# Square into a spent tile, first state over ScalarE and GpSimd, a third output tile

## The chip, the cores and the metric

The kernel runs on one core of a Trainium2 chip. Its engines work from queues of their own and wait for each other by semaphores: TensorE (PE) multiplies matrices, VectorE (DVE) and ScalarE (ACT) work on rows of SBUF and PSUM, GpSimd (POOL) on SBUF alone in this kernel, and SyncE (SP) issues every transfer. The metric is the device time of one execution in microseconds (us).

## The reference

Three stages follow each other, on 4 batches of 768 positions:

- Gated linear attention, 8 heads of 48: `state = alpha[t] * state + k[t] v[t]^T`, `y[t] = q[t] state`.
- A spectral mix: `theta = x @ w_theta`, `zr = x cos(theta)`, `zi = x sin(theta)`, `y = w_tok_r zr + w_tok_i zi` over positions, `u = x + y`, then `u + relu(u @ w_ch)`. Width 384.
- A gated convolution: `h = relu(x @ w_in)` (1024 wide), a depthwise convolution of three taps over positions, a sigmoid gate, and `(h * gate) @ w_out`.

All is in float32, and the weights are stored as 64-bit words.

## The kernel before

**Attention.** Positions are cut into 6 chunks of 128 per batch, 24 chunks in all. For each chunk DVE makes products of decay factors: a backward scan (line 210) and, from its inverse at the chunk's start, a forward scan (line 215), both into one tile `fbt`, of which there is one. Line 218 multiplies them into q and k. ScalarE then squares the tile in place (line 219) for the sake of a row sum, `bacc`, with which the kernel later finds whether any factor overflowed. The decay factors come in a tile `a_t`, of which there are two; nothing reads its first 512 columns after the forward scan. `ftot`, four numbers a row (line 216), is the chunk's whole decay.

TensorE makes the scores `sc`, ScalarE copies them into `pt` (line 232), GpSimd masks them (line 233), TensorE makes `y` from pt and v and, from the second chunk of a batch on, from the running state `S`. `kv` (line 264) is the chunk's own addition to the state. From the second chunk on, DVE sums S and kv into `tst` (line 268) and GpSimd multiplies with the next chunk's decay (line 273), in two instructions, one for either half of the heads. In a batch's first chunk there is no sum, and DVE multiplies kv straight out of PSUM. Two state tiles alternate. `x` is the copy of y, `xps` and `u` its transpose.

**Spectral mix.** `th` is theta; its chain runs over ScalarE and DVE (lines 310 to 315) to the tile `zf`, which is split in a high part `zh` (ScalarE) and a low part `zl` (DVE, line 72), since each product of matrices is done in three passes of such halves (`mm3`). The mix `yps` of a batch takes 18 matmuls for each of 6 chunks and each half of the positions; the token weights of the first half are `wtok00`, `wtok01`, those of the second `wtok10`, `wtok11`. The matmuls of a batch's mix stand among those of the next batch's attention. For batch 0 there is no earlier mix to fill in.

**Weights.** Each piece of a weight is loaded into a tile `stage` (two of them), decoded by DVE (lines 101 to 103) and split: the cast by ScalarE (line 71), the rest by DVE (line 72). w_theta takes two pieces, w_tok 12, of which the first six are the first half of the positions.

**Last stage.** `hps`, `ops` and `cps` are the products with w_in, w_out and w_ch. ScalarE copies each finished output into a tile `ob` (line 492), of which there are two, and SyncE stores it.

**The order.** It is not written out by hand: the program is handed to a scheduler, which simulates a timeline of it and sets each engine's queue by that. Each engine then goes through its queue in order. An edit of one instruction so moves others on all engines.

Of the kernel before, what the change touches and what calls it, by code (L numbers as in the profile page):

```python
# [8 lines left out]
F32 = mybir.dt.float32  # L9
F32R = mybir.dt.float32r  # L10
BF16 = mybir.dt.bfloat16
# [3 lines left out]
AF = mybir.ActivationFunctionType  # L15
# [3 lines left out]
P = 128  # L19
B, H, S, D = 4, 8, 768, 48  # L20
DM = H * D
# [7 lines left out]
CW = 4 * P  # L29
# [14 lines left out]
def tile_gated_linear_attention__then__spectral_moe__then__conv_gate(  # L44
# [14 lines left out]
    nc = tc.nc  # L59
    NCH = B * NC  # L60

    def mm(o, lhsT, rhs, start, stop):
        nc.tensor.matmul(o, lhsT, rhs, start=start, stop=stop, skip_group_check=True)  # L63

    def mm3(o, a, b, start, stop):
        mm(o, a[0], b[0], start, False)
        mm(o, a[0], b[1], False, False)
        mm(o, a[1], b[0], False, stop)
# [8 lines left out]
    bacc = top_p.tile([P, NCH], F32, name="bacc")  # L77
# [7 lines left out]
    def body(top, slow):  # L85
# [38 lines left out]
        with ExitStack() as ph1:  # L124
# [73 lines left out]
            def a_prep(ci):  # L198
                at, qt, vt = raw.pop(ci)
                qr = qt[:, 0:CW]  # L200
                kr = qt[:, CW : 2 * CW]
                ff = at[:, 0:CW]
                ash = at[:, 1 : CW + 1]
                ast = at[:, CW + 1 : CW + 5]
                fbt = sc_p.tile([P, 2, CW], F32, tag="fbt", name="fbt")
                fo, bf = fbt[:, 0], fbt[:, 1]
                bt = bf.rearrange("p (a t) -> p a t", a=4)
                of = onehot.rearrange("p a t -> p (a t)")
                ftot = att.tile([P, 4], F32, tag="ftot", name="ftot")
                nc.vector.tensor_tensor_scan(  # L210
                    bf[:, CW - 1 :: -1], ash[:, CW - 1 :: -1], of[:, CW - 1 :: -1], 0.0, ALU.mult, ALU.add
                )
                nc.vector.tensor_scalar(starts[:, :, 0], bt[:, :, 0], LEAST, None, ALU.max)
                nc.vector.reciprocal(starts[:, :, 0], starts[:, :, 0])
                nc.vector.tensor_tensor_scan(fo, ff, starts.rearrange("p a t -> p (a t)"), 0.0, ALU.mult, ALU.add)  # L215
                nc.vector.tensor_tensor(ftot, ast, bt[:, :, 0], ALU.mult)
                fl = fbt.rearrange("p b t -> p (b t)")
                nc.vector.tensor_tensor(qt, qt, fl, ALU.mult)  # L218
                nc.scalar.activation(fl, fl, AF.Square, accum_out=bacc[:, ci : ci + 1])  # L219
                prep[ci] = (qr.rearrange("p (a t) -> p a t", a=4), kr.rearrange("p (a t) -> p a t", a=4), ftot, vt)  # L220

            def a_score(ci):
# [21 lines left out]
            def a_y(ci):  # L244
                qh, kh, ftot, vt = prep.pop(ci)
                pts, kt = scored.pop(ci)
                c = ci % NC
                Sp, Sn = Sst[ci % 2], Sst[(ci + 1) % 2]
                y = ps_a.tile([P, DM], F32, tag="a", name="y")
                first = True  # L250
                for p in range(NP):
                    for j in range(2):
                        h = 2 * p + j
                        mm(y[:, h * D : (h + 1) * D], pts[j][:, p, :], vt[:, h * D : (h + 1) * D], first, c == 0)
                        first = False
                    if c > 0:
                        mm(y[:, p * 96 : p * 96 + 96], qh[:, p, :], Sp[:, p, :], False, True)
                x = x_p.tile([P, DM], F32, tag="x", name="x")
                nc.scalar.copy(x, y)
                xs[ci] = x  # L260
                if c < NC - 1:
                    kv = ps_a.tile([P, NP, 2 * D], F32, tag="a", name="kv")
                    for p in range(NP):
                        mm(kv[:112, p, :], kt[:, p, :112], vt[:, p * 96 : p * 96 + 96], p == 0, True)
                    nft = prep[ci + 1][2]
                    if c > 0:
                        tt = att.tile([P, NP, 2 * D], F32, tag="tst", name="tst", bufs=1)
                        nc.vector.tensor_tensor(tt[:112], Sp[:112], kv[:112], ALU.add)
                    else:
                        tt = kv  # L270
                    for j in range(2):
                        r = slice(64 * j, 64 * j + D)
                        (nc.gpsimd if c > 0 else nc.vector).tensor_tensor(  # L273
                            Sn[r, :, j * D : (j + 1) * D],
                            tt[r, :, j * D : (j + 1) * D],
                            nft[r].unsqueeze(2).to_broadcast([D, NP, D]),
                            ALU.mult,
                        )
# [64 lines left out]
            def a_att(b, c):  # L343
                ci = b * NC + c
                if slow:
                    xs[ci] = x_p.tile([P, DM], F32, tag="x", name="x")
                    nc.sync.dma_start(out=xs[ci], in_=x_dram[b, c * P : (c + 1) * P, :])
                    a_xt(ci)
                    return
                if ci + 2 < NCH:  # L350
                    a_load(ci + 2)
                if ci + 1 < NCH:
                    a_prep(ci + 1)
                    a_score(ci + 1)
                a_y(ci)
                a_xt(ci)

            if not slow:
                a_load(0)
                a_load(1)  # L360
                wps = ps_a.tile([P, 512], F32, tag="a", name="wps")
                for _ in range(NWARM):
                    nc.tensor.matmul(wps, onehot[:, 0, :], onehot.rearrange("p a t -> p (a t)"), start=True, stop=True)
                a_prep(0)
                a_score(0)
# [79 lines left out]
        mlp = top.enter_context(tc.tile_pool(name="mlp", bufs=2))  # L445
# [39 lines left out]
        def m_out(b, h, i):  # L485
            ps = ps_n.tile([P, 512], F32, tag="n", name="ops")
            ts_ = slice(i * P, (i + 1) * P)
            for f in range(NF):
                g = gsp[b, h, f]
                mm3(ps[:, :DM], (g[:, 0, ts_], g[:, 1, ts_]), (wout[0][:, f, :], wout[1][:, f, :]), f == 0, f == NF - 1)  # L490
            ob = mlp.tile([P, DM], F32, tag="ob", name="ob")
            nc.scalar.activation(ob, ps[:, :DM], AF.Copy, scale=0.5)
            t0 = h * HALF + i * P
            nc.sync.dma_start(out=out[b, t0 : t0 + P, :], in_=ob)
# [43 lines left out]
        for n, (b, h) in enumerate(units):  # L538
            if n > 0:
                m_xsplit(b, h)  # L540
            for f in range(NF):
                m_in(b, h, f)
                if n > 0 and f in (1, 3, 5):
                    m_out(*units[n - 1], f // 2)
                i = NF * n + f - 2 * NF
                if not slow and i % 2 and 0 <= i // 2 < NTOP:
                    top_min(i // 2)
                if f == 6 and n + 2 < len(units):
                    m_usplit(*units[n + 2])
                    m_ch(*units[n + 2], ps_m, "m")  # L550
            if n == 7 and not slow:
                count_bad()
        for i in range(3):
            m_out(*units[-1], i)
# [102 lines left out]
```

## Time and profile before

| | us |
|---|---|
| median of 3 runs | 613.31 |
| lowest, highest run | 610.01, 613.78 |
| the profiled execution, its own time | 610.02 |
| its span, first to last instruction | 608.3 |
| PE busy | 584.0 (96%) |
| DVE busy | 459.9 (76%) |
| ACT busy | 333.3 (55%) |
| POOL busy | 71.1 (12%) |

Shares are means over stages that differ. The profile tells the busy time of each engine by stretches of the span, the chain of work that ended last, what each engine waited for, and groups of instructions by line, operation and shape. A matmul in float32 appears as two in the trace. The granted clock is TensorE's, 1.00 being 2.4 GHz.

### The profile page before, as it was taken

The page shows a single profiled execution, that of the slowest core. Times are in us where ns is not written, and L with a number is a line of the kernel's source. Part 1 is how long each engine was busy: PE and PEld are TensorE (multiplying, and loading weights), DVE is VectorE, ACT ScalarE, POOL GpSimd, SP SyncE. Part 2 cuts the span into 40 slices and gives each one's busy share as a digit, 9 for nine tenths or more (in the row PEclk, how much of TensorE's full clock was granted, in tenths as well). Part 3 has the DMA queues.
Part 4 walks back from the last instruction along what each step waited for, and adds up shares of the span by engine and source line. Part 5 has one row for each costly group of instructions (what it writes and reads, how often), then busy time and mean ns, then how long its engine had stood idle before and what let it go on. Part 6 is the DMA issues. An engine that isn't in the chain of part 4 may idle for free.

```text
span 608.3 us, 9546 instructions
## 1 busy us (share of the span) xinstructions
PE 584.0 (96%) x3703; PEld 569.2 (94%) x3703; DVE 459.9 (76%) x744; ACT 333.3 (55%) x663; POOL 71.1 (12%) x91
## 2 busy tenths in 40 slices
PE   5789999899999999999999999999999999999996
PEld 2689888799999999999999999999999999999995
DVE  7699999976764567643156888998888888888781
ACT  3436766444682446733265343666776767766571
POOL 1023621432001330112100000000000000000000
PEclk8557899899999999999999999999999999999999
DMA  8356464343102431021001333430023535445111
GB/s 297 116 176 215 151 222 127 125 138 112 62 19 77 131 119 48 15 66 61 1 0 74 110 106 105 122 138 13 27 79 117 194 118 182 148 152 194 55 41 44
DMA packets 24981, 65.33 MB, mean 107 GB/s; under 512 B 2528, under 2 KB 8672, under 8 KB 24544
## 3 DMA queue, kind: packets, MB, share of 16 engines
q1 hardware_dynamic: 24928, 64.64, 32.3%
q8 instruction: 31, 0.51, 0.3%
q14 instruction: 22, 0.18, 0.1%
HBM read 59.92 MB, written 4.72 MB: 106 GB/s over the span
## 4 chain that ended last, share of the span: by engine, by line
PE 83%; DVE 11%; DMA 2%; issue 1%; ACT 1%; POOL 1%; ACTq 0%; DVEq 0%
PE yps L63 23%; PE hps L63 17%; PE ops L63 16%; PE y L63 8%; PE cps L63 6%; PE th L63 5%; PE sc L63 3%; PE kv L63 2%; DMA stage<-in_w_tok_dram 2%; DVE fbt L215 2%; DVE fbt L210 1%; PE kps L239 1%; DVE qk_t L218 1%; DVE stage L102 1%; DVE wtok L72 1%
## 5 line engine op out<-in xcount | busy, mean ns | idle before, releaser
L63 PE MATMUL yps<-wtok,zh 128*128 128x384 f32 x576 | 151.6, 343 | 1.0 <-ACT zh L71 1.0
L63 PEld LDWEIGHTS yps<-wtok,zh 128*128 128x128 f32 x576 | 105.9, 192 | 1.7 <-ACT zh L71 1.4
L63 PE MATMUL hps<-x,win 128*128 128x386 f32 x576 | 107.1, 339 | 0.0
L63 PE MATMUL ops<-wout,g 128*128 128x384 f32 x576 | 106.9, 338 | 0.0
L63 PEld LDWEIGHTS hps<-x,win 128*128 128x128 f32 x576 | 102.2, 189 | 0.0
L63 PEld LDWEIGHTS ops<-wout,g 128*128 128x128 f32 x576 | 101.7, 187 | 0.0
L63 PE MATMUL yps<-wtok,zl 128*128 128x384 f32 x288 | 97.9, 344 | 0.0
L233 POOL TENSOR_SCALAR_AFFINE_SELECT pt<-pt 128x512 f32<-128x512 f32 x48 | 46.0, 981 | 214.9 <-ACT pt L232 214.9
L63 PE MATMUL y<-v_t,pt 128*128 128x48 f32 x384 | 59.2, 286 | 0.0
L63 PEld LDWEIGHTS y<-v_t,pt 128*128 128x128 f32 x384 | 56.3, 213 | 0.5
L63 PEld LDWEIGHTS yps<-wtok,zl 128*128 128x128 f32 x288 | 55.2, 192 | 0.0
L219 ACT ACTIVATE fbt<-fbt 128x1024 f32<-128x1024 f32 x24 | 25.4, 1059 | 52.8 <-DVE qk_t L218 52.5
L479 ACT ACTIVATE cv<-cv 128x384 f32<-128x384 f32 x64 | 33.4, 523 | 31.0 <-DVE cv L476 30.9
L72 DVE TENSOR_TENSOR g<-cv,g 128x384 fp32r<-128x384 f32 x64 | 35.4, 555 | 15.1 <-ACT g L71 14.5
L63 PE MATMUL th<-wth,zh 128*128 128x384 f32 x216 | 44.3, 348 | 0.0
L232 ACT COPY pt<-sc 128x512 f32<-128x512 f32 x48 | 25.7, 585 | 29.7 <-PE y L63 29.7
L210 DVE TENSOR_TENSOR_SCAN fbt<-a_t,onehot 128x512 f32<-128x512 f32 x24 | 29.7, 1236 | 16.3 <-ACT fbt L219 14.4
L63 PEld LDWEIGHTS sc<-qk_t 48*128 48x128 f32 x384 | 28.6, 204 | 14.0 <-issue 7.5
L63 PE MATMUL sc<-qk_t 48*128 48x128 f32 x384 | 33.8, 304 | 8.0 <-DVE qk_t L218 8.0
L473 DVE SCALAR_TENSOR_TENSOR cv<-hh,cw,cv 128x383 f32<-128x383 f32 (+1 forms) x64 | 38.3, 612 | 4.1 <-ACT cv L470 3.8
L63 PE MATMUL y<-S,qk_t 128*128 128x96 f32 x160 | 37.5, 319 | 3.9 <-POOL S L273 3.9
L480 DVE SCALAR_TENSOR_TENSOR cv<-cv,hh 128x384 f32<-128x384 f32 x64 | 35.2, 555 | 7.9 <-ACT cv L479 5.9
(84 smaller groups left out, 903.5 us busy)
## 6 DMA issues: line engine op xcount, KB each, us to landing
qk_t<-in_qka_dram SPq DMA_DIRECT2D x24, 512.0 KB, 3.7
stage<-in_w_tok_dram SPq DMA_DIRECT2D x12, 768.0 KB, 4.9
top<-in_w_tok_dram SPq DMA_DIRECT2D x12, 768.0 KB, 4.3
a_t<-in_qka_dram SPq DMA_DIRECT2D x24, 260.0 KB, 2.8
v_t<-in_v_dram SPq DMA_DIRECT2D x24, 192.0 KB, 3.3
out_dram<-ob SPq DMA_DIRECT2D x24, 192.0 KB, 1.9
stage<-in_w_in_dram SPq DMA_DIRECT2D x4, 768.0 KB, 5.1
stage<-in_w_out_dram SPq DMA_DIRECT2D x4, 768.0 KB, 4.3
```

The lines of the kernel that those rows point to most:

```text
L63: nc.tensor.matmul(o, lhsT, rhs, start=start, stop=stop, skip_group_check=True)
L72: lo_eng.tensor_tensor(lo, src, hi.bitcast(F32), ALU.subtract)
L102: nc.vector.scalar_tensor_tensor(fb, hi, 0xC0000000, fb, ALU.bitwise_and, ALU.bitwise_or)
L210: nc.vector.tensor_tensor_scan(bf[:, CW - 1 :: -1], ash[:, CW - 1 :: -1], of[:, CW - 1 :: -1], 0.0, ALU.mult, ALU.add)
L215: nc.vector.tensor_tensor_scan(fo, ff, starts.rearrange("p a t -> p (a t)"), 0.0, ALU.mult, ALU.add)
L218: nc.vector.tensor_tensor(qt, qt, fl, ALU.mult)
L219: nc.scalar.activation(fl, fl, AF.Square, accum_out=bacc[:, ci : ci + 1])
L232: nc.scalar.copy(pt, scs[j])
L233: nc.gpsimd.affine_select(pt, pt, [[0, NP], [1, P]], ALU.is_ge, 0.0, base=0, channel_multiplier=-1)
L473: nc.vector.scalar_tensor_tensor(cv[:, a:HALF], hh[:, o + a - 1 : o + HALF - 1], cw[:, f, 0:1], cv[:, a:HALF], ALU.mult, ALU.add)
L479: nc.scalar.activation(cv, cv, AF.Tanh, scale=0.5)
L480: nc.vector.scalar_tensor_tensor(cv, cv, 1.0, hh[:, o : o + HALF], ALU.add, ALU.mult)
```

## The change

Three edits. The Square writes its result, which nobody reads, as bfloat16 into the first 512 columns of `a_t`, and stands ahead of the product with q and k; both now only read `fbt`. In a batch's first chunk ScalarE copies the two blocks of kv into the state tile, and GpSimd multiplies them there in place. `ob` has three tiles.

```diff
@@ a_prep
                 fl = fbt.rearrange("p b t -> p (b t)")
+                sink = at[:, 0:CW].bitcast(BF16)
+                nc.scalar.activation(sink, fl, AF.Square, accum_out=bacc[:, ci : ci + 1])
                 nc.vector.tensor_tensor(qt, qt, fl, ALU.mult)
-                nc.scalar.activation(fl, fl, AF.Square, accum_out=bacc[:, ci : ci + 1])
@@ a_y
                     else:
-                        tt = kv
+                        tt = Sn
+                        for j in range(2):
+                            r = slice(64 * j, 64 * j + D)
+                            nc.scalar.copy(Sn[r, :, j * D : (j + 1) * D], kv[r, :, j * D : (j + 1) * D])
                     for j in range(2):
                         r = slice(64 * j, 64 * j + D)
-                        (nc.gpsimd if c > 0 else nc.vector).tensor_tensor(
+                        nc.gpsimd.tensor_tensor(
@@ m_out
-            ob = mlp.tile([P, DM], F32, tag="ob", name="ob")
+            ob = mlp.tile([P, DM], F32, tag="ob", name="ob", bufs=3)
```

In the changed kernel the product of line 218 is line 220; the lines behind it are one higher, and four higher from the state products (now line 277) on. On DVE, the opening of batch 0, from the third chunk's reciprocal on, stood so before:

```order
L273 TENSOR_TENSOR S1_112<-kv_234,ftot_192 48x4x48 x2
L215 SCALAR_TENSOR_TENSOR fbt_276<-a_t_185,starts_110 128x512
L72 TENSOR_TENSOR wth1_116<-stage_247,wth0_115 128x768
L218 TENSOR_TENSOR qk_t_187<-qk_t_187,fbt_276 128x1024
L72 TENSOR_TENSOR wth1_116<-stage_255,wth0_115 128x384
L72 TENSOR_TENSOR zh_344<-u_241,zh_344 128x384
L210 SCALAR_TENSOR_TENSOR fbt_373<-a_t_270,onehot_109 128x512
```

and stands so now:

```order
L215 SCALAR_TENSOR_TENSOR fbt_278<-a_t_185,starts_110 128x512
L220 TENSOR_TENSOR qk_t_187<-qk_t_187,fbt_278 128x1024
L72 TENSOR_TENSOR wth1_116<-stage_249,wth0_115 128x768
L210 SCALAR_TENSOR_TENSOR fbt_375<-a_t_272,onehot_109 128x512
L213 TENSOR_SCALAR starts_110<-fbt_375 128x4
L216 TENSOR_TENSOR ftot_376<-a_t_272,fbt_375 128x4
L72 TENSOR_TENSOR wth1_116<-stage_257,wth0_115 128x384
```

The state products are gone; the product with q and k stands ahead of the split of the theta weights, and the next chunk's scan right behind that split. On ScalarE the queue now reads there, from the first chunk's kt on:

```order
L242 COPY kt_183<-kps_178 128x512
L242 COPY kt_221<-kps_216 128x512
L274 COPY S1_112<-kv_234 48x4x48 x2
L115 ACTIVATE stage_249<-stage_249 128x768
L233 COPY pt_210<-sc_200 128x512
L233 COPY pt_213<-sc_201 128x512
L260 COPY x_232<-y_223 128x384
L71 CAST wth0_115<-stage_249 128x768
L115 ACTIVATE stage_257<-stage_257 128x384
L219 ACTIVATE a_t_185,bacc_61<-fbt_278 128x1024
```

Before, the cast of the theta weights stood between the two pt, two places behind the scaling of line 115; now kt, both copies into the state, both pt and x stand ahead of it. The third place is DVE in the middle of batch 0, from chunk 0's zl on. Before:

```order
L72 TENSOR_TENSOR zl_364<-zf_357,zh_344 128x768
L216 TENSOR_TENSOR ftot_568<-a_t_464,fbt_567 128x4
L72 TENSOR_TENSOR zh_538<-u_241,zh_538 128x384
L311 SCALAR_TENSOR_TENSOR zf_454<-zf_454,th_444 128x384
L218 TENSOR_TENSOR qk_t_466<-qk_t_466,fbt_567 128x1024
L101 TENSOR_SCALAR stage_621<-stage_621 128x768
L101 TENSOR_SCALAR stage_709<-stage_709 128x768
L102 SCALAR_TENSOR_TENSOR stage_621<-stage_621 128x768
L315 TENSOR_TENSOR zf_454<-x_321,zf_454 128x768
```

Now:

```order
L72 TENSOR_TENSOR wtok01_85<-stage_436,wtok00_84 128x2x384
L103 SCALAR_TENSOR_TENSOR stage_533<-stage_533 128x768
L72 TENSOR_TENSOR zl_366<-zf_359,zh_346 128x768
L72 TENSOR_TENSOR wtok01_85<-stage_533,wtok00_84 128x2x384
L101 TENSOR_SCALAR stage_623<-stage_623 128x768
L102 SCALAR_TENSOR_TENSOR stage_623<-stage_623 128x768
L269 TENSOR_TENSOR tst_427<-S0_111,kv_422 112x384
L103 SCALAR_TENSOR_TENSOR stage_623<-stage_623 128x768
L101 TENSOR_SCALAR stage_711<-stage_711 128x768
L216 TENSOR_TENSOR ftot_570<-a_t_466,fbt_569 128x4
L102 SCALAR_TENSOR_TENSOR stage_711<-stage_711 128x768
L72 TENSOR_TENSOR wtok01_85<-stage_623,wtok00_84 128x2x384
```

Where the theta chain of chunk 1 (lines 311 and 315, zf_454) stood right behind chunk 0's zl, the decodes of the fifth and sixth piece of w_tok (stage_623, stage_711) stand now, and the theta chain behind them.

## Rows read from the trace of the kernel before

**Rows 1.** Busy us (count) by stretch: PE, PEld, DVE, ACT, POOL; granted clock, DMA share, GB/s.

```profile
40.00:60.00 20.00, 20.00 (x118) 18.97 (x117) 19.59 (x29) 11.85 (x23) 7.15 (x6) 0.67 0.77 254
...
100.00:120.00 20.00, 17.46 (x138) 16.51 (x138) 19.89 (x29) 9.87 (x19) 7.27 (x6) 0.95 0.46 139
120.00:300.00 180.00, 180.00 (x1338) 174.56 (x1336) 105.81 (x158) 89.18 (x173) 35.07 (x52) 0.99 0.23 72
```

**Rows 2.** The chain that ended last: start us, us, what.

```profile
17.93 2.91 PE y L63 x14
...
99.36 1.03 PE kv L63 x8
...
103.57 2.83 PE y L63 x24
...
107.19 3.18 PE yps L63 x18
...
112.13 0.56 DVE tst L268
...
112.77 2.69 POOL S L273
...
116.69 3.55 PE y L63 x20
```

**Rows 3.** Waits of DVE, 0 to 40 us: us in total, times, longest.

```profile
DVE stage L101 <- DMA stage<-in_w_tok_dram: 1.7, 1, 1.7
DVE fbt L210 <- ACT fbt L219: 1.5, 2, 1.2
```

**Rows 4.** DVE in order of time: start us, us, instruction, idle before and releaser.

```profile
21.77 0.72 DVE L273 TENSOR_TENSOR S<-kv,ftot 48x192 f32<-48x192 f32 x2 [3.24 <-PE kv L63]
```

**Rows 5.** ACT by form, 0 to 120 us: busy us, mean ns, idle before and releaser.

```profile
L219 ACT ACTIVATE fbt<-fbt 128x1024 f32<-128x1024 f32 x10 | 10.6, 1058 | 26.6 <-DVE qk_t L218 26.6
...
L241 ACT COPY kt<-kps 128x512 f32<-128x512 f32 x8 | 4.8, 597 | 1.5 <-PE kps L239 1.1 <-PE kv L63 0.4
L259 ACT COPY x<-y 128x384 f32<-128x384 f32 x8 | 3.9, 489 | 0.0
...
L71 ACT CAST wth<-stage 128x768 fp32r<-128x768 f32 x1 | 0.8, 835 | 0.0
```

**Rows 6.** DVE by form, 0 to 120 us.

```profile
L210 DVE TENSOR_TENSOR_SCAN fbt<-a_t,onehot 128x512 f32<-128x512 f32 x11 | 13.7, 1245 | 3.4 <-DMA a_t<-in_qka_dram 1.9 <-ACT fbt L219 1.5
L103 DVE SCALAR_TENSOR_TENSOR stage<-stage 128x768 uint32<-128x768 uint32 x13 | 12.6, 973 | 0.0
...
L102 DVE SCALAR_TENSOR_TENSOR stage<-stage 128x768 uint32<-128x768 uint32 x13 | 12.5, 960 | 0.0
L72 DVE TENSOR_TENSOR wtok<-stage,wtok 128x768 fp32r<-128x768 f32 x11 | 11.5, 1048 | 0.0
L101 DVE TENSOR_SCALAR stage<-stage 128x768 uint32<-128x768 uint32 x13 | 7.8, 607 | 2.0 <-DMA stage<-in_w_tok_dram 2.0
L72 DVE TENSOR_TENSOR zl<-zf,zh 128x768 fp32r<-128x768 f32 x6 | 6.7, 1112 | 0.0
...
L273 DVE TENSOR_TENSOR S<-kv,ftot 48x192 f32<-48x192 f32 x4 | 1.4, 353 | 3.3 <-PE kv L63 3.2
```

**Rows 7.** DMA issues: KB each, median us from issue to landing.

```profile
stage<-in_w_tok_dram SPq DMA_DIRECT2D x12, 768.0 KB, 4.9
```

**Rows 8.** POOL by form, 0 to 120 us.

```profile
L273 POOL TENSOR_TENSOR S<-tst,ftot 48x192 f32<-48x192 f32 x10 | 11.8, 1184 | 7.8 <-DVE tst L268 7.2
```

**Rows 9.** The end, ACT in order of time.

```profile
600.62 0.87 ACT L492 ACTIVATE ob<-ops 128x384 f32<-128x384 f32 x2 [5.15 <-PE ops L63]
603.10 0.49 ACT L492 ACTIVATE ob<-ops 128x384 f32<-128x384 f32 x1 [1.60 <-DMA out_dram<-ob]
```

**Rows 10.** Stretches of 5 us, columns as in rows 1.

```profile
70.00:75.00 5.00, 5.00 (x22) 5.00 (x22) 4.97 (x8) 3.83 (x7) 2.09 (x2) 0.51 0.85 231
...
120.00:125.00 5.00, 5.00 (x22) 5.00 (x21) 4.96 (x6) 2.92 (x6) 4.32 (x4) 0.53 0.60 199
```

## The prediction

> **What bounds the kernel now.** I read the stretches first, then the chain of waits, then what each engine waited for in the opening, then the order of the instructions.
>
> The table of stretches splits the run in two. From 40 to 60 us VectorE (DVE) is busy 19.59 of 20 us, and from 100 to 120 us 19.89 of 20; the two stretches between read the same. From 120 to 300 us TensorE (PE) is busy all 180 us and DVE only 105.81 [rows 1]. So up to about 117 us, while batch 0 runs its recurrence and the weights are decoded, DVE sets the pace; behind it TensorE works off a queue that never empties. The end is then (time at which TensorE stops waiting for DVE) + (work left on TensorE) + (tail). The chain shows where that hand-over is: DVE's state sum of batch 1, chunk 1 (tst) at 112.13, the state products on GpSimd (POOL) from 112.77, and the y that uses the state at 116.69 [rows 2]. After that the chain is TensorE's until 600.6. Nothing that the change does between 120 and 600 us can count, unless it makes TensorE wait there.
>
> **The opening: waits that go, waits that come.** With the old order the second chunk's first scan waits for the Square of the first, because the Square rewrites the tile in place; the two such waits in the first 40 us cost 1.5 [rows 3], of which I take 1.2 for the first. Now Square and product read the tile side by side, and that 1.2 goes. The two state products leave DVE, and with them its wait of 3.24 for kv [rows 4]. The first token-weight stage, for which DVE waited 1.7 [rows 3], is asked for earlier and needed later: 1.7 goes. Together 6.1.
>
> What is late next? The instruction that DVE now reaches is the split of the theta weights, which waits for ScalarE's (ACT) cast of them. DVE came free at 21.77 - 3.24 = 18.53 [rows 4]; less 1.2, plus a scan and a product, 1.25 each by the scan's row [rows 6], it is there at 19.8. The four kv end at 21.7 now; the new order puts all of them ahead of seven y, which took 2.91 [rows 2], and starts 1.2 sooner: 17.6. Behind kv ScalarE does kt (0.60), the two new copies, a scaling as long as the cast (0.84), two pt (0.60 each), x (0.49), the cast (0.84) [rows 5]. A copy of 48x192 has no row; it lies between nothing and the 0.49 of x, which has twice the columns, and I take 0.35. That is 4.7, so the cast ends at 22.3 and DVE waits 2.4. The scan behind it needs the third Square, queued on ScalarE behind the cast and another scaling: 22.3 + about 0.5 + 1.06 [rows 5] = 23.9, against 22.3 + 0.9 for DVE: 0.7. So 6.1 - 3.1: **3.0 gained**, with bounds 0 (ScalarE later still) and 6.1.
>
> **The order on DVE after that.** The scheduler lays out the whole program again, and this is the larger term. Before the tst that hands over, the new order has, beside what stood there before, two more weight splits (2 x 1.05), one line-102 step (0.96), two line-103 steps (2 x 0.97), one line-101 step (0.61), one scan (1.25), and it lacks four state products (4 x 0.353) [rows 6]: 6.86 - 1.41 = **5.4 lost**. These are decodes of the second half of the token weights, which nobody needs before 117 us, and DVE has no idle time that could take them [rows 1]. The zl of batch 0 show the same: the second now has two more weight splits and most of two more decodes ahead of it. Bounds: 0, if TensorE is not waiting there, and 5.4.
>
> In the same place two w_tok stages follow each other so closely that the fifth can be asked for only when the third is split, with a line-103 step (0.97), a zl split (1.11) and a weight split (1.05) [rows 6] before its first decode: 3.1 against 4.9 from issue to landing [rows 7]. **1.8 lost** (0 to 1.8).
>
> TensorE has four more mix matmuls behind it at the hand-over, which is 4 x 3.18/18 [rows 2]: **0.7 gained**.
>
> **States of later batches, and the Square.** Per batch two products of 0.353 leave DVE, two copies of about 0.35 go to ScalarE, and two products to GpSimd, at 1.18 each in the first 120 us [rows 8]. In batch 1 TensorE ends kv at 99.36 + 1.03 and begins the y that uses the state at 103.57 [rows 2], 3.2 later, with six mix matmuls between; the new order has twelve there, 6 x 0.18 more, so 4.2. The new path is kt's copy, two copies and two products, 0.6 + 0.7 + 2.4 = 3.7. Covered, barely: nothing in the sum, and up to 2.0 if the products run long. The next load into the decay tile now waits for the Square rather than the scan, about 1.1 later, and the loads behind it on SyncE move with it; they are for two chunks on, so nothing.
>
> A rule of the Trainium skill speaks against this part: SBUF — State Buffer, section Who interferes with whom, says that a VectorE instruction with two SBUF inputs contends with a GpSimd instruction that reads SBUF, and that the loser is blocked for the whole instruction. The trace agrees in kind: the first product of the hand-over takes 2.69 [rows 2], against a mean of 1.18. By that rule two products that each wait for a 1.25 instruction would be 2.5 longer, the path 6.2 against 4.2 of cover, and the sum by it 2.0 more, 613.9 in place of 611.9.
>
> **Tail.** The last three outputs are copied at 600.62 (two) and 603.10, the third after 1.60 of waiting for the first one's store [rows 9]. All three stand in the same order now, and with a third tile nothing holds the last: **1.6 gained**. Bounds 0 (three stores at once slow each other) and 1.6.
>
> **Sum.** -3.0 + 5.4 + 1.8 - 0.7 - 1.6 = +1.9 on the profiled execution's own 610.0: 611.9. The three runs shown are 610.0, 613.3 and 613.8, so that execution lies with the lowest, and a median lies 0 to 3.3 above it; I add the middle, 1.6: **613.5**, no change that can be told. About 1%, 6.1 us, is what can be told from none.
>
> **Rivals.**
>
> *The order's price is not paid.* TensorE was itself busy through 40 to 60 us at a granted clock of 0.67 [rows 1], and may be the one that sets the pace; then later decodes cost nothing and the opening and the tail remain: -3.0 - 0.7 - 1.6 = -5.3, 604.7, or 601.6 with all of the 6.1. Against it: DVE at 99% [rows 1], and the 3.9 from 112.77 to 116.69 in which the chain stands on GpSimd and TensorE's y has to wait [rows 2].
>
> *The lower clock of TensorE (slower).* The granted clock falls to half (1.2 of 2.4 GHz) when TensorE has waited: 0.51 from 70 to 75 us, 0.53 from 120 to 125, the second right behind the wait for the state [rows 10]. That second stretch, 5 us, cost about 2.3, since TensorE was by then the bound. The mix of four chunks now gets its zl later. If each of three more of them leaves such a stretch that DVE's work doesn't cover, 6.9 comes on top: 618.8. It decides once TensorE waits over 2 us at several zl instead of at one state. Against it: the stretch at 70 us was hidden behind DVE.
>
> *The Square still holds the scan.* The scan still waits for ScalarE, in queue order; if the Square sits behind other work there, the opening gives nothing: +4.9, 614.9.
>
> **How the numbers follow.** Forecast 0.52, the order's price not paid 0.18 (of which a third below 604), the lower clock 0.14, the Square 0.12, anything else 0.04. The forecast with its bounds (-3 to +8 on 610.0) and the Square's case lie within 1% of before nearly always; of the first rival about half lies below, of the clock's case about two thirds above. With the 0 to 3.3 of the runs added, the range that holds 8 in 10 goes from 606 (the first rival in the middle of the runs) to 620 (the clock's case a little above its own 618.8). Faster by over 1%: 0.09. Slower by over 1%: 0.12. Within: 0.79.
>
> **What would show it.** Right: DVE's wait for kv in the first 40 us gone and a wait for the cast of the theta weights in its place; a wait of DVE for a w_tok stage between 50 and 62 us; the tst of batch 1, chunk 1, 3 to 5 us later than 112.13; the last ob copied without waiting. Wrong: that tst at or before 112, a third half-clock stretch past 100 us, or any wait of TensorE after 130 us.

## The result, and the profile after

| | before | after |
|---|---|---|
| median of 20 runs, us | 612.16 | 615.91 |
| lowest, highest | 609.16, 615.25 | 610.91, 618.55 |
| span of the profiled execution | 608.3 | 611.2 |

After to before is 1.0059 [1.0040, 1.0078]: a loss of 0.6%, within the 1% that was forecast, 2.4 us above the 613.5.

The stretches of the changed kernel, with the columns of [rows 1]:

```profile
40.00:60.00 20.00, 18.56 (x116) 17.72 (x115) 16.96 (x26) 9.13 (x16) 3.19 (x5) 0.73 0.59 180
100.00:120.00 20.00, 16.71 (x135) 15.55 (x134) 19.93 (x26) 11.31 (x23) 7.18 (x8) 1.00 0.30 106
120.00:300.00 180.00, 178.54 (x1338) 173.19 (x1338) 103.07 (x155) 90.20 (x178) 33.66 (x57) 0.99 0.23 72
65.00:70.00 5.00, 3.71 (x13) 3.31 (x13) 5.00 (x7) 4.44 (x10) 2.18 (x2) 0.50 0.82 272
120.00:125.00 5.00, 4.39 (x29) 4.39 (x30) 4.90 (x9) 1.52 (x3) 0.55 (x1) 0.75 0.28 67
125.00:130.00 5.00, 5.00 (x31) 4.80 (x32) 1.31 (x4) 3.81 (x8) 2.19 (x4) 0.91 0.37 130
```

From 40 to 60 us VectorE is no longer full: 16.96 of 20, where it had 19.59. What it waited for, from 0 to 40 us and then from 40 to 125 us (us in total, times, longest):

```profile
DVE fbt L210 <- DMA a_t<-in_qka_dram: 1.9, 1, 1.9
...
DVE stage L101 <- DMA stage<-in_w_tok_dram: 0.3, 1, 0.3
DVE stage L101 <- DMA stage<-in_w_theta_dram: 0.3, 1, 0.3
...
DVE stage L101 <- DMA stage<-in_w_tok_dram: 4.8, 4, 2.0
DVE ftot L216 <- POOL S L277: 2.0, 2, 1.0
```

The waits for the Square and for kv are gone from the opening [rows 3, 4]; new ones stand behind 40 us, for weights that have not landed and for GpSimd. The hand-over, on VectorE, GpSimd and TensorE in order of time:

```profile
117.84 0.52 DVE L269 TENSOR_TENSOR tst<-S,kv 112x384 f32<-112x384 f32 x1
...
118.45 2.10 POOL L277 TENSOR_TENSOR S<-tst,ftot 48x192 f32<-48x192 f32 x2 [1.61 <-DVE starts L213]
...
120.61 0.46 PE L63 MATMUL y<-S,qk_t 128*128 128x96 f32 x2 [1.05 <-POOL S L277]
```

Against [rows 2], tst is 5.7 later and the y behind it 3.9. The third piece is the end, on ScalarE:

```profile
603.52 0.87 ACT L496 ACTIVATE ob<-ops 128x384 f32<-128x384 f32 x2 [5.16 <-PE ops L63]
605.28 0.49 ACT L496 ACTIVATE ob<-ops 128x384 f32<-128x384 f32 x1 [0.89 <-PE ops L63]
```

The last copy waits for TensorE's products now, no longer for a store [rows 9], and yet the span ends 2.9 later, as TensorE's last matmul does.

### The profile page after: what moved, and what is told of

The parts are those of the page before. It is cut to its first block, busy times and chain, and to the rows that moved or that the text cites. A ratio compares the mean times of both kernels' runs of the same rounds, so it can differ in the third digit from the quotient of the medians.

```text
span 611.2 us, 9585 instructions
## 1 busy us (share of the span) xinstructions
PE 581.6 (95%) x3703; PEld 564.5 (92%) x3703; DVE 455.9 (75%) x736; ACT 335.3 (55%) x671; POOL 70.4 (12%) x99
## 4 chain that ended last, share of the span: by engine, by line
PE 55%; DVE 8%; issue 6%; DMA 4%; ACT 1%; SPq 0%; POOLq 0%; DVEq 0%; ACTq 0%
PE ops L63 17%; PE hps L63 14%; PE yps L63 10%; PE y L63 5%; PE cps L63 3%; PE sc L63 2%; DMA stage<-in_w_in_dram 2%; PE th L63 2%; PE kv L63 1%; DVE stage L103 1%; DVE stage L102 1%; PE kps L240 1%; DMA stage<-in_w_out_dram 1%; DMA qk_t<-in_qka_dram 1%; DVE us L72 1%
## 5 line engine op out<-in xcount | busy, mean ns | idle before, releaser
L63 PEld LDWEIGHTS yps<-wtok,zh 128*128 128x128 f32 x576 | 104.6, 190 | 4.6 <-ACT zh L71 3.4
L63 PE MATMUL yps<-wtok,zl 128*128 128x384 f32 x288 | 96.3, 340 | 0.7 <-DVE zl L72 0.7
L234 POOL TENSOR_SCALAR_AFFINE_SELECT pt<-pt 128x512 f32<-128x512 f32 x48 | 41.4, 884 | 210.3 <-ACT pt L233 210.3
L219 ACT ACTIVATE a_t<-fbt 128x1024 bf16<-128x1024 f32 x24 | 25.4, 1058 | 55.2 <-DVE fbt L215 49.2
L63 PE MATMUL cps<-us,wch 128*128 128x384 f32 x216 | 40.2, 338 | 1.3 <-DVE u L428 1.3
L63 PEld LDWEIGHTS th<-wth,zh 128*128 128x128 f32 x216 | 39.9, 200 | 0.0
L220 DVE TENSOR_TENSOR qk_t<-qk_t,fbt 128x1024 f32<-128x1024 f32 x24 | 29.6, 1232 | 13.4 <-DMA qk_t<-in_qka_dram 13.1
L474 ACT ACTIVATE cv<-hh,cw 128x384 f32<-128x384 f32 x64 | 38.1, 615 | 2.8 <-DVE g L72 2.4
L63 PEld LDWEIGHTS cps<-us,wch 128*128 128x128 f32 x216 | 38.1, 188 | 1.6 <-ACT us L71 1.6
```

What stands on the lines that cost most here:

```text
L219: nc.scalar.activation(sink, fl, AF.Square, accum_out=bacc[:, ci : ci + 1])
L234: nc.gpsimd.affine_select(pt, pt, [[0, NP], [1, P]], ALU.is_ge, 0.0, base=0, channel_multiplier=-1)
L474: nc.scalar.activation(cv, hh[:, o : o + HALF], AF.Copy, scale=cw[:, f, 1:2])
```

## The experiments

Each ran beside the kernel before, on one chip with it. In short, with the time of tst of batch 1, chunk 1, in the profiled execution:

| kernel | median us | ratio to before | tst at |
|---|---|---|---|
| third output tile alone | 613.53 | 1.0015 [0.9987, 1.0043] | 112.9 |
| Square alone | 605.3 | 0.9905 [0.9883, 0.9927] | 107.74 |
| state alone | 607.68 | 0.9937 [0.9914, 0.9960] | 109.73 |
| Square and state | 615.07 | 1.0062 [1.0037, 1.0088] | 117.99 |
| change, late decodes behind chunk 3's zl | 614.67 | 1.0013 [0.9975, 1.0050] | 115.44 |
| change, behind chunk 5's zl | 620.28 | 1.0131 [1.0090, 1.0171] | 115.29 |
| before, behind chunk 5's zl | 613.24 | 1.0000 [0.9970, 1.0029] | 110.28 |
| Square alone, behind chunk 4's zl | 611.98 | 0.9990 [0.9972, 1.0009] | 110.45 |
| change, first half's decodes spread | 611.83 | 1.0002 [0.9974, 1.0030] | 111.89 |
| before, the same | 609.68 | 0.9977 [0.9943, 1.0011] | 113.61 |
| before, two state products on VectorE | 611.10 | 1.0001 [0.9974, 1.0029] | 115.98 |
| change, the same | 610.34 | 0.9968 [0.9945, 0.9991] | 118.66 |

The last column is read from one execution of each kernel, and it moves without any change of order. VectorE's order up to tst is the same, instruction for instruction, in the kernel before, with the third tile alone, and with the state products moved in the kernel before; tst stands there at 112.1, 112.9 and 116.0. It is one order, too, in the change, in Square and state, and in the change with the products moved: 117.8, 118.0 and 118.7. So a difference below 4 us in this column need not come from the order. Nor is tst the time: the last of these has the latest tst of all and is 5.6 us faster than the change.

### One part at a time

The third output tile alone:

```diff
-            ob = mlp.tile([P, DM], F32, tag="ob", name="ob")
+            ob = mlp.tile([P, DM], F32, tag="ob", name="ob", bufs=3)
```

> The kernel before with three output tiles and nothing else; DVE's queue is as before. Theory A (the tail of the prediction): the third output copy no longer waits 1.60 us for a store, so the time falls by 1.6 us. Rival B (from the trace of the change, where the last copy ends 0.5 us behind the last matmul and the span still ends 5.9 us behind it, as before): TensorE's last matmul and what follows it set the end, so the copy comes earlier and the time changes by 0 to -0.8 us.

The last copies, ScalarE in order of time:

```profile
601.67 0.87 ACT L492 ACTIVATE ob<-ops 128x384 f32<-128x384 f32 x2 [5.16 <-PE ops L63]
603.43 0.49 ACT L492 ACTIVATE ob<-ops 128x384 f32<-128x384 f32 x1 [0.89 <-PE ops L63]
```

The wait for the store is gone and no gain can be seen (rival B; the interval reaches from a gain of 0.8 us to a loss of 2.6). Most of the wait of 1.60 had covered another, for the last products themselves: the third copy begins 1.76 behind the first in this kernel and 2.48 behind it in [rows 9], so the tile freed 0.7 at most. In this execution the last store then gave it back: from issue to landing it took 3.7 us, and 3.8 in the change, against 3.2 in the kernel before. In three later kernels with three tiles it took 1.9 to 2.0. What sets this, no run here shows.

The Square alone:

```diff
+                sink = at[:, 0:CW].bitcast(BF16)
+                nc.scalar.activation(sink, fl, AF.Square, accum_out=bacc[:, ci : ci + 1])
                 nc.vector.tensor_tensor(qt, qt, fl, ALU.mult)
-                nc.scalar.activation(fl, fl, AF.Square, accum_out=bacc[:, ci : ci + 1])
```

> The kernel before with the Square alone moved into the spent tile. DVE's queue up to the tst of batch 1, chunk 1 differs from before by one scan more (+1.25 us). Theory A (it is the order on DVE that costs, and both edits together bring it): the Square's wait goes (-1.2), the scan comes (+1.25), tst within 1.5 us of 112.13, time within 2 us of before. Rival B (the Square between the scans and ScalarE's other work is what costs): tst 2 to 4 us later and the time 2 to 3 us up, as in the whole change.

This part alone gains 1%. Neither theory had that: A set the time within 2 us of before, B 2 to 3 above it. Its stretches, columns as in [rows 1]:

```profile
0.00:50.00 50.00, 37.95 (x226) 31.62 (x227) 45.28 (x69) 25.30 (x46) 13.31 (x20) 0.76 0.67 223
50.00:100.00 50.00, 46.00 (x322) 43.61 (x322) 47.98 (x69) 31.33 (x59) 18.93 (x15) 0.93 0.54 172
100.00:160.00 60.00, 57.58 (x426) 54.28 (x425) 46.42 (x68) 29.48 (x57) 16.16 (x18) 1.00 0.35 112
```

The same stretches of the kernel before:

```profile
0.00:50.00 50.00, 37.28 (x187) 31.92 (x187) 39.95 (x61) 20.41 (x37) 8.15 (x18) 0.62 0.57 192
50.00:100.00 50.00, 46.91 (x326) 44.52 (x326) 49.93 (x70) 32.71 (x62) 20.45 (x16) 0.90 0.58 185
100.00:160.00 60.00, 57.46 (x426) 55.51 (x426) 48.45 (x70) 28.68 (x56) 18.94 (x20) 0.94 0.41 126
```

VectorE did 45.28 us of work in the first 50 instead of 39.95. TensorE was busy as long as before, but at 0.76 instead of 0.62. Busy time by granted clock adds up to 129 us of full-clock work by 160 us, against 119 before; the span is 7.5 shorter. TensorE's idle time in these 160 us is the same, 18.5 and 18.4. So in this pair of executions the gain is clock, not less waiting: the first stretch at the lower clock ended at 37.4 us here and at 53.0 before. Why it ended sooner is not shown.

The state alone (the hunk of a_y in the change, nothing else):

> The kernel before with the first state by ScalarE copies and GpSimd products alone. DVE's queue up to the tst of batch 1, chunk 1 has four state products less (-1.41 us) and one line-103 step more (+0.97). Theory A (order): with the 3.2 us wait for kv gone and the queue no longer, tst comes 1 to 4 us earlier than 112.13 and the time falls by 1 to 4 us. Rival B (the products on GpSimd are what costs, 2.2 us against 0.7 on DVE): the first y with the state is late in every batch, the time is 2 to 3 us up, as in the whole change.

Theory A held, at the upper end of its range: tst is 2.4 earlier, and the time 4.0 lower.

Square and state, without the third output tile:

> The change without the third output tile: DVE's queue is that of the whole change. Theory A: both edits bring the long queue (+5.4 us ahead of that tst) and the stage waits: tst at 117 to 119 us, time 2 to 4 us up, 1.003 to 1.007 of before, the same as the whole change within 0.8 us. Rival B (edits add up): the sum of what the Square alone and the state alone give, whatever these are; under A those two are 0 and -1 to -4 and do not add up to this.

The numbers are those of theory A, and the edits do not add up: beside a median of before of 611.73, the two halves gain 6.4 and 4.0, and together they lose 3.3. What the two together have and neither half has is another order from the scheduler. In either half alone VectorE's work ahead of tst, counted by [rows 6], is within 1.3 of the kernel before; in both together it is 5.5 more. Whether this work is what costs, the next runs ask.

### Is it the work ahead of the hand-over?

If so, taking decodes from in front of tst should give the time back. The decodes of the second half's token weights were held behind a given split of batch 0's theta chain:

```diff
-                        load_tok(1, c)
+                        with tc.issue_after(last_zl[NC - 3].ins):
+                            load_tok(1, c)
```

NC - 3 is chunk 3; NC - 1 and NC - 2 make the others. `last_zl` holds each chunk's split, counted through all batches, so these are batch 0's chunks (not batch 1's, as the first expectation has it).

> The whole change, and VectorE's decodes of the second half's token weights may not stand ahead of the theta split of chunk 3 of batch 1 (counted by the rows' means, 108.4 us of VectorE work stand ahead of the sum tst of batch 1 chunk 1, against 116.4 in the changed kernel and 110.9 in the one before). Theory A (what the changed kernel loses is VectorE work that was moved ahead of that sum): tst comes at 109 to 112 instead of 117.8, TensorE's end 4 to 8 us earlier than in the changed kernel, time 608 to 612. Theory B (the time is set behind the hand-over, by ScalarE and TensorE's own work, and the order at VectorE only moves waits): tst comes early, but the time stays within 2 us of the changed kernel's 616. Theory C (the later decodes make the second half's scores wait): a TensorE wait for a second-half token weight of over 3 us shows, and the time is above 617.

> The same with the decodes behind the theta split of chunk 5, the last of the first half (102.7 us of VectorE work ahead of the sum tst). Theory A: tst at 104 to 107, or as far as the kv matmuls let it, and time 603 to 609. Theory B: within 2 us of 616. Theory C, the likelier here than with chunk 3: the last decode of the second half's token weights has 132 us of VectorE work up to it, so their first user waits 3 us or more, and the time is no better than with chunk 3.

> The kernel before, with the same rule as the last (105.1 us of VectorE work ahead of the sum tst instead of 110.9). Theory A: tst at 106 to 109 instead of 112.1, and time 3 to 6 us under the kernel before, though neither Square nor state were touched. Theory B: within 2 us of the kernel before.

> The kernel before with the Square into the spent tile alone, and the decodes behind the theta split of chunk 4 (105.1 us of VectorE work ahead of the sum tst against 112.2 with the Square alone, whose tst came at 107.7 and whose time was 605.3). Theory A: tst at 101 to 105, time 599 to 604. Theory B, that at 107.7 the sum was no longer what TensorE waited for: within 2 us of 605.3. Theory C: 607 or more, with a TensorE wait for second-half token weights.

Theory A fell in all four: no time came down to where it had it. The rule of chunk 3 came nearest, with 614.67, but its interval overlaps that of the change without a rule. Up to tst, the kernel with the rule of chunk 3 had these stretches (columns as in [rows 1]):

```profile
0.00:40.00 40.00, 27.44 (x143) 23.16 (x144) 33.54 (x50) 18.32 (x34) 10.08 (x19) 0.64 0.61 200
40.00:115.44 75.44, 67.69 (x452) 63.40 (x451) 64.47 (x92) 43.34 (x82) 18.27 (x21) 0.85 0.48 151
```

the changed kernel these:

```profile
0.00:40.00 40.00, 29.13 (x148) 23.72 (x149) 35.08 (x50) 18.97 (x35) 12.49 (x20) 0.67 0.63 214
40.00:117.84 77.84, 68.24 (x467) 63.15 (x468) 71.89 (x98) 45.20 (x83) 22.71 (x21) 0.89 0.53 166
```

and the kernel before these:

```profile
0.00:40.00 40.00, 27.29 (x141) 22.58 (x142) 30.36 (x47) 14.75 (x26) 6.94 (x16) 0.65 0.52 177
40.00:112.13 72.13, 69.04 (x466) 65.28 (x465) 71.57 (x100) 45.86 (x85) 25.13 (x20) 0.86 0.62 195
```

The rule took 7.4 us of work from VectorE behind 40 us, 71.89 to 64.47, and VectorE's idle time there rose from 5.95 to 10.97. Five of the seven came back as waits: for GpSimd, for q and k, for ScalarE's half of the theta chain, for kv. That is more than executions of one order differ by: the idle time there is 0.6 to 3.8 in the three kernels with the order of before, and 5.7 to 6.4 in the three with that of the change. I read it so that without the rule the decodes fill such gaps; no run shows this by itself. Behind the hand-over the delayed decodes then met the next states. TensorE's wait in that kernel, and the clock around it (us, PE busy, granted clock, DMA share, GB/s):

```profile
131.87 0.74 PE L63 MATMUL y<-S,qk_t 128*128 128x96 f32 x2 [2.21 <-POOL S L277]
...
130.00:135.00 5.00, 3.13 (x15) 0.58 0.22 57
```

With the rule of chunk 5 it is two such waits:

```profile
118.69 0.46 PE L63 MATMUL y<-S,qk_t 128*128 128x96 f32 x2 [1.79 <-POOL S L277]
144.22 0.73 PE L63 MATMUL y<-S,qk_t 128*128 128x96 f32 x2 [2.70 <-POOL S L277]
```

With the Square alone the rule threw away nearly all that the Square had gained: tst went from 107.74 to 110.45 with less work ahead of it, and the next state cost this, TensorE in order of time and then the stretch behind it:

```profile
124.18 0.74 PE L63 MATMUL y<-S,qk_t 128*128 128x96 f32 x2 [2.09 <-POOL S L274]
...
125.00:130.00 5.00, 5.00 (x27) 0.50 0.51 176
```

In the kernel before, the rule of chunk 5 changed nothing (1.0000), as theory B had it: tst came 1.9 earlier, and TensorE waited 2.2 and 2.5 us for two later states. Theory B's time held with chunk 3 in the change as well. In the other two, theory C had the right kind of cost, decodes too late, at the wrong place: no wait for a token weight shows; the state products do.

### Is it the crowding in the middle of batch 0?

The changed kernel's stage waits of 2.01 and 0.85 stand at 53.6 and 57.3 us, where pieces follow each other every few us. Here a piece of the first half, from chunk 3 on, is held behind an earlier zl:

```diff
-                load_tok(0, c)
                 if c > 0:
                     a_theta(c - 1)
+                if c > 2:
+                    with tc.issue_after(last_zl[c - 2 - 1].ins):
+                        load_tok(0, c)
+                else:
+                    load_tok(0, c)
```

> The whole change, and the piece of the first half's token weights for chunk c (c above 2) may not be decoded ahead of the theta split zl of chunk c-3 of batch 0. By the rows' means the second zl has 58.7 us of VectorE work ahead of it instead of 71.2, the hand-over's sum tst 104.9 instead of 116.4, and between a stage's split and its next decode lie 9.9, 13.3 and 21.7 us instead of 5.5, 3.1 and 3.1; the last decode of the second half ends at 126 instead of 115. Theory D (the changed kernel loses in the middle of batch 0, where two pieces of token weights follow each other faster than their transfers land and hold the theta chains queued behind them on VectorE and ScalarE): VectorE's waits for a stage between 40 and 70 us fall from 3.7 to under 1.5, TensorE's waits for x, zh and zf between 50 and 70 us from 8 to under 3, and the time to 603 to 609. Theory B (the time is set behind that, by clock and hand-over): these waits go, the time stays at 612 to 617. Theory C (decodes still in progress at 126 take it back): a TensorE wait behind 117 us of over 3 us.

> The kernel before, with the same rule on the first half's token weights (second zl at 59.5 instead of 62.8, sum tst at 110.4 instead of 110.9 of VectorE work). Theory D: the stage waits were small here already, so the time is within 3 us of the kernel before. Theory E (the rule itself gains, whatever Square and state do): as much below the kernel before as the last run lies below the changed one.

In the changed kernel this gave 0.6% back, just to the time of before; the intervals of this run and of the change do not overlap. In the kernel before it gave 0.2%, which can't be told from none. So the crowding may be a part of the loss (theory D), but a smaller one than D said, which had 603 to 609. Theory E, that the rule gains in either kernel alike, is not excluded: the gains of 0.6% and 0.2% lie closer together than their intervals are wide. In the changed kernel VectorE's waits from 40 to 70 us have no stage among them any more:

```profile
DVE ftot L216 <- POOL S L277: 2.3, 3, 1.0
DVE zf L319 <- ACT zf L318: 1.6, 1, 1.6
DVE zf L315 <- ACT zf L314: 1.2, 1, 1.2
DVE wtok L72 <- ACT wtok L71: 0.9, 1, 0.9
```

tst stands at 111.89, 6 us earlier than in the change, and even so the hand-over is late. The chain of this kernel:

```profile
112.51 3.09 POOL S L277
...
115.66 1.14 POOL S L277
...
116.86 0.64 POOL pt L234
...
117.54 5.60 PE y L63 x24
```

The two state products took 4.2 us, and the mask of the next scores, queued behind them on GpSimd, let TensorE wait 2.4.

### The state products at the hand-over

The last pair leaves VectorE's order ahead of tst as it was and takes two chunks' products from GpSimd. In the changed kernel:

```diff
-                        nc.gpsimd.tensor_tensor(
+                        (nc.vector if NC < ci < NC + 3 else nc.gpsimd).tensor_tensor(
```

> The kernel before, with the state products of batch 1's chunks 1 and 2 on VectorE instead of GpSimd; VectorE's order ahead of the hand-over's sum tst is unchanged. In the kernel before, the two GpSimd products behind that sum took 4.0 us in all and TensorE waited 2.5 us for them, with a half-clock stretch of 5 us behind the wait. Theory F (part of the price of the hand-over is the two slow products on GpSimd, and the half clock that the wait brings): tst where it was (111 to 114), the y that uses the state within 2 us of tst's start instead of 4.6, no wait of TensorE there, the half clock behind it gone, time 3 to 6 us below the kernel before. Theory G (a product on VectorE delays the decodes behind it, and the next state or the last zl split waits instead): within 2 us of the kernel before.

> The changed kernel with the same edit. There the two products took 2.25 us and TensorE waited 1.05 us for them, with a clock of 0.75 and 0.91 in the ten us behind. Theory F: y within 2 us of tst, time 1 to 4 us below the changed kernel's 615.9, still above the kernel before with the same edit by the 3 to 4 us that the order of the decodes costs. Theory G: within 2 us of the changed kernel.

In the changed kernel it gained 5.6 on the medians (the intervals 0.9968 [0.9945, 0.9991] and 1.0059 [1.0040, 1.0078] do not meet), more than theory F said, though tst is no earlier. F had the order still cost 3 to 4 us against the kernel before with the same edit; that did not come, the two cannot be told apart. With the products out of the way, the 5 us of work more ahead of tst cost nothing that can be seen. VectorE in order of time, and the stretches behind (all engines, as in [rows 1]):

```profile
118.66 0.52 DVE L269 TENSOR_TENSOR tst<-S,kv 112x384 f32<-112x384 f32 x1
119.65 0.71 DVE L277 TENSOR_TENSOR S<-tst,ftot 48x192 f32<-48x192 f32 x2
...
120.00:125.00 5.00, 5.00 (x46) 4.89 (x43) 4.88 (x8) 1.15 (x2) 0.00 (x0) 1.00 0.11 13
125.00:130.00 5.00, 4.18 (x26) 3.70 (x24) 4.72 (x10) 3.13 (x7) 1.44 (x2) 1.00 0.62 212
```

From 110 to 200 us TensorE waits 0.8 in all, and the clock stays at its full level. In the kernel before the same edit gained nothing, as theory G had it: the products stood 2.4 behind tst in VectorE's queue, TensorE's wait there was halved but not gone (1.27, before 2.54), and another stood further on, at a chunk whose products were left on GpSimd. VectorE, GpSimd and TensorE:

```profile
115.98 0.56 DVE L268 TENSOR_TENSOR tst<-S,kv 112x384 f32<-112x384 f32 x1
118.93 0.69 DVE L273 TENSOR_TENSOR S<-tst,ftot 48x192 f32<-48x192 f32 x2
...
119.67 0.46 PE L63 MATMUL y<-S,qk_t 128*128 128x96 f32 x2 [1.27 <-DVE S L273]
138.23 1.33 POOL L273 TENSOR_TENSOR S<-tst,ftot 48x192 f32<-48x192 f32 x2 [1.61 <-DVE tst L268]
139.61 0.70 PE L63 MATMUL y<-S,qk_t 128*128 128x96 f32 x2 [0.75 <-POOL S L273]
```

The granted clock is 1.00 behind the first of these waits and 0.50 behind the last, from 140 to 145 us.

No kernel that was tried beats the Square alone, which beats both.

## Why the prediction was right, and where it was not

**Which way, and how much.** Forecast: no change that can be told, 613.5. Measured: 615.91, no change by that bound. But of its terms only the order came out at its size; the opening, the stage wait, the tail and the stretch from tst to the end did not, with both signs. That the sum came as near as 2.4 us is in part luck.

**The opening, 3.0 gained.** VectorE's idle time in the first 40 us fell from 9.64 to 4.92, from the busy times shown: 4.7 gained. The waits that go were read rightly. The new wait for the cast of the theta weights, 2.4, did not come, nor the 0.7 behind it for the third Square. ScalarE's cast and VectorE's split:

```profile
20.02 0.86 ACT L71 CAST wth<-stage 128x768 fp32r<-128x768 f32 x1
...
21.14 1.38 DVE L72 TENSOR_TENSOR wth<-stage,wth 128x768 fp32r<-128x768 f32 x1
```

ScalarE had kv in hand at 16.2, not 17.6, and did both copies into the state in 0.65 rather than 0.70; the cast began at 20.02, and VectorE came to the split only at 21.14. The bound of 6.1 held.

**The order on VectorE, 5.4 lost.** VectorE's busy time ahead of tst is 106.97 against 101.93: 5.0. The size was right. The meaning given to it was not: that VectorE sets the pace to 117 us, so that work ahead of tst is time lost. Less work there left most of itself behind as idle time, and with the products moved the same work ahead of tst cost nothing that can be seen. VectorE was full, but it was not alone the bound: the waits that appear when its work is taken away are for the theta chain through ScalarE, for kv, for q and k, and for the states through GpSimd.

**The stage wait, 1.8 lost.** The longest is 2.0, in the place that was named:

```profile
53.60 0.56 DVE L101 TENSOR_SCALAR stage<-stage 128x768 uint32<-128x768 uint32 x1 [2.01 <-DMA stage<-in_w_tok_dram]
```

There were three more, 4.8 in all, and 1.0 for GpSimd at 74.7 (the other 1.0 for GpSimd ends at 40.1 and falls into the opening). This is the term that was mis-sized most: idle time behind 40 us rose by 5.4 (0.56 to 5.95). One of the three kernels with the order of before had 3.84 there, so a part of this rise may be the execution and not the change. Together, -4.7 + 5.0 + 5.4 = +5.7, which is how much later tst is. The forecast's own terms gave +4.2: 1.7 more was gained in the opening, 0.4 less was lost to the order, 3.6 more to waits.

**From tst to the end.** From the first product to y it is 2.2 against 3.9 [rows 2], so y is only 3.9 later, and TensorE ends 2.9 later. The four mix matmuls done earlier are 0.7 of the difference, at the prediction's price. The half-clock stretch behind y is shallower, 0.75 and 0.91 [rows 10: 0.53]; new waits of 2.1 past 125 us go the other way. The rest I have not taken apart.

**States of later batches: nothing, as forecast.** The first pair behind the copies of batch 1 took 1.72, not the 2.4 that the prediction allowed, and TensorE did not wait for it; the 2.0 that the long products could have added did not come.

```profile
108.45 1.72 POOL L277 TENSOR_TENSOR S<-S,ftot 48x192 f32<-48x192 f32 x2 [2.45 <-ACT S L274]
```

**The tail, 1.6 gained: wrong.** The step read a wait that was ended by a store as time that would vanish. The last copy needs the last products too, which leaves 0.7 to gain, and the last store took 0.6 longer, as the prediction's lower bound of 0 allowed. In the changed kernel the span ends 5.9 behind TensorE's last matmul (592.25 + 12.99 us), and 6.0 before (589.36 + 12.99). The tile alone, with an interval of -0.8 to +2.6 us, shows no gain.

**The signs named.** The kv wait was gone, but no wait for the cast of the theta weights stood in its place. The stage wait came, tst was 5.7 later (3 to 5 were named), and the last ob had no store to wait for. Of the wrong ones, a wait of TensorE behind 130 us came: 1.3 for u of a later stage and 0.9 for u of a mix, with no clock lost.

**The rivals.** The Square still holding the scan: refuted by the Square alone, 0.9905, and no wait for a Square in the trace. The lower clock: from 100 to 120 us TensorE waited 2.1 for a zh and 0.7 for a zl, nearly as that rival wanted, and the granted clock stayed at 1.00. The fall in the middle of batch 0 came as before, 0.50 from 65 to 70 us [rows 10: 0.51 from 70 to 75]. The order's price not being paid is undecided in that form: spreading the decodes gave back 3.5 us, moving the late ones away 2.8 in one place, with overlapping intervals, and a further loss in the other. That the two orders cannot be told apart once the products are moved (0.9968 and 1.0001, with intervals that overlap) speaks for it.

**GpSimd beside VectorE.** A state product of one shape takes 0.497 to 3.620 us in the changed kernel, and a pair at VectorE's side 0.71. With VectorE idle beside it a product took 0.50; the longest, 3.62 at 70.4 us, ran beside four instructions of VectorE without a gap and ended 0.4 behind the last. With two pairs moved there, TensorE's wait at the hand-over and the clock's fall behind it were gone. The Trainium skill, SBUF — State Buffer, section Who interferes with whom, holds that the two engines share a port pair and lock each other out; the long products agree with that in kind, and no run here separates the port from other causes.

**What stays open.** Why the two halves lose together is shown as far as this: the layout of both exposes the products at the hand-over (moving them gives 0.9%, and nothing in the kernel before), and it crowds the weights in batch 0 (spreading them gives 0.6% back; that the kernel before gains less by it is not shown). The two were not tried together, and neither reaches the 1.6% between the Square alone and the change. Nor is it shown why the Square alone ran at the higher clock sooner.

## What to carry to other kernels

Where a scheduler lays out the whole program again, run each part of a change alone: here two parts worth 1.0% and 0.6% made a loss of 0.6%. An engine at 99% busy may be filled rather than bound; take a little work away from it and see whether the hand-over comes earlier or idle time appears, before pricing every instruction in front of it. Where one landmark of a trace (here tst) stands for the time, look first how far it moves between executions of one order. And before a wait is counted as a gain, look for what would end next at the same place: the wait for a store covered most of the wait for the last products.

## What the runs showed of the hardware

The kernel before, run 98 times beside these experiments, spreads with TensorE's mean granted clock: 36 runs at 0.957 or more have a median of 610.3 us, 37 at 0.951 or less one of 614.2. A line through all runs of all kernels, each about its own mean, gives 3.1 us for 0.01. It does not say which of the two causes the other. By it, as an estimate, half of what the Square alone gained goes with a higher clock (0.966 against 0.955 in the mean) and half does not; of the 4.9 us between the means of the change and of its version with the products on VectorE, 1.6 goes with the clock.

In each of the 14 profiled executions, TensorE's last matmul ends at its idle time, plus half of its busy time at the lower clock (0.50 in these traces), which is what that clock cost it, plus 559 to 563 us. The kernel before idled 18.3 us and lost 23.8 to the clock; the change 23.7 and 20.4; the Square alone 18.6 and 13.2; the third tile alone, with the order of before, 24.7 and 17.3. So more waiting need not cost time, and the two are best read together.
